# The masks of both halves of a unit's scores in one piece on the vector engine, behind the last score

## The chip, the cores and the metric

The kernel runs on one core of a Trainium2 chip. Its five engines run side by side, each through its own list of instructions: TensorE (PE, with its weight loads shown apart as PEld), VectorE (DVE), ScalarE (ACT), GpSimd (POOL) and SyncE (SP, which issues most DMAs). The metric is the time of one execution on the device, in microseconds (us).

## The reference

Three stages follow one another. The first is a linear recurrence with a complex decay, the second a gated product layer without a nonlinearity, the third eight experts of which each token takes one or none.

```python
def _attn_ref(q, k, v, a_re, a_im):             # (4, 8, 768, 48) each
    mag = np.sqrt(a_re * a_re + a_im * a_im)
    scale = np.minimum(mag, 0.999) / (mag + 1e-06)
    a_re_n, a_im_n = a_re * scale, a_im * scale
    for t in range(S):
        ar, ai = a_re_n[:, :, t, :, None], a_im_n[:, :, t, :, None]
        new_re = ar * S_re - ai * S_im
        new_im = ar * S_im + ai * S_re
        kv = np.einsum('bhd,bhe->bhde', k[:, :, t], v[:, :, t])
        S_re, S_im = new_re + kv, new_im
        y[:, :, t] = np.einsum('bhd,bhde->bhe', q[:, :, t], S_re)
    return y

def _moe_ref(x, w_a, w_b, w_out):               # (3072, 384), 384 x 1536, 1536 x 384
    return (x @ w_a) * (x @ w_b) @ w_out

def _moe2_ref(x, w_skip, w_gate, w1, w2):       # 8 experts, 384 -> 1024 -> 384
    out = x.copy(); do_compute = x @ w_skip > 0; xc = x[do_compute]
    e_idx = np.argmax(xc @ w_gate, axis=1)      # gate_w is the softmax weight of e_idx
    for e in range(E):
        mask = e_idx == e
        y[mask] = gate_w[mask, None] * (np.maximum(xc[mask] @ w1[e], 0.0) @ w2[e])
    out[do_compute] = xc + y
    return out
```

## The kernel before, in words

The recurrence is cut into 24 units: six chunks c of 128 tokens by four batch rows, in the order of `units`. A unit's decays are turned into running products (logarithms on ACT, sums by triangular matmuls `l` on PE, lines L197 and L198, exponentials on ACT), with which q and k are scaled on DVE and POOL (`qr`, `kr`). L323 and L330 transpose them on PE into `pq` and `pk`, which ACT copies into `tq` and `tk`, each in two halves hh of four heads.

`att_run` does the rest of a unit. All its matmuls go through the helper `run` (L368), which ties each to the one before, so their order on PE is fixed among themselves, while other work may stand between them. In order: eight score matmuls of half 0 into `pc`, eight of half 1; the update `ds` of the state, unless c is the last chunk; then `y`, pair of heads by pair: two matmuls with the state (not at c = 0) and two with the masked scores `sc`, the first two pairs from half 0, the last two from half 1. The masks are three DVE instructions for each half: L387 multiplies the right halves of all score blocks by the triangle, L388 the upper left quarter (64 partitions) of the even heads, L389 the lower one of the odd heads; they write `sc0` and `sc1`. A matmul of an even head needs L387 and L388 of its half, one of an odd head needs L389 as well.

The second stage goes on beside it. Two units make a group of 256 tokens, and each group has twelve steps: 18 matmuls `ab` (L562 to L564), a copy on ACT and a product on DVE (`asb`, L568 and L569), a rounded part on ACT and its remainder on DVE (`gh`, `gl`, L571 and L573), and `op` (L545 to L547). The weights of that stage arrive as raw 64-bit words and are decoded at the start, in eighteen chunks (names da, db, do in START): ACT `abs` L431, DVE L432, L436 and L437, ACT L442 and POOL L443.

What sets the order: the program is written in one sequence, and a scheduler with a model of times puts each engine's instructions in order by priority when it builds the kernel; on the chip each engine runs its list in that order and waits with a semaphore where an operand is missing. Three things overrule the scheduler. START lists the steps of the startup, HOLD ties some instructions behind marked ones (the masks are marked ("sc", unit, half)), and whatever is inside `tc.high_priority()`, as the three masks are (L386), is placed as early as its operands allow in that model.

Of the kernel before, what the change touches and what calls it, by code (L numbers as in the profile page):

```python
# [15 lines left out]
ALU = mybir.AluOpType  # L16
AX = mybir.AxisListType

P = 128
# [39 lines left out]
def kern(tc, q, k, v, a_re, a_im, w_a, w_b, w_out, w_skip, w_gate, w1, w2, out):  # L59
    nc = tc.nc  # L60
    dve, act, pool, pe, sync = nc.vector, nc.scalar, nc.gpsimd, nc.tensor, nc.sync
    st = ExitStack()
    with st:
# [13 lines left out]
        def at(name):  # L77
            env.n += 1
            return bank(env.at[env.n % len(env.at)], name, 2)
# [8 lines left out]
        tri = tri_r.bitcast(F32)  # L88
# [15 lines left out]
        for b in range(B):  # L104
            s_ = cpool.tile([96, H * D + 16], F32, name=f"state{b}")
# [16 lines left out]
        tri2 = ew.tile([P, 2, 64], BF16, name="tri2", tag="tri2", bufs=1)  # L122
# [3 lines left out]
        scs = [ew.tile([P, 4, P], F32, name=f"sc{hh}", tag=f"sc{hh}", bufs=1) for hh in range(2)]  # L126
        for s_ in scs:
            s4 = s_.rearrange("s (j x) t -> s j x t", x=2)
# [12 lines left out]
        def after(later, earlier, how=mybir.DependencyClass.NoSync):  # L141
            tc.add_manual_dep(
                later, earlier.name,
                mybir.DependencyInfo(how, mybir.DependencyReason.DATA),
                reason="table order",
            )
# [4 lines left out]
        def mark(key, i):  # L151
            marks[key] = i.ins
            return i
# [143 lines left out]
        def att_pe(i):  # L297
            env.net = None
            att_turn(i)
            att_run(i)  # L300
            env.row = None
# [36 lines left out]
        def att_run(i):  # L338
            c, b = units[i]
            d = U[i]  # L340
            kr, vt, ee = d["kr"], d["v"], d["ee"]
            qT, tks, vp, last, copied = d["turned"]
            if env.net is not None:
                last = env.net
            sc = []
            stt = state[b]

            def delta(run):

                ds = at(f"ds{i}")  # L350
                for h in range(H):
                    for x in range(2):
                        l = d["kf"][:, 96 * h + 64 * x : 96 * h + 64 * x + 64]
                        run(ds[64 * x : 64 * x + 64, h * D : (h + 1) * D], l, vt[:, h * D : (h + 1) * D], start=True, stop=True)
                return ds

            def new_state(ds):
                s3 = stt[:, :W].rearrange("p (h e) -> p h e", e=D)
                d3 = ds[:96, :W].rearrange("p (h e) -> p h e", e=D)
                if c > 0:  # L360
                    dve.tensor_tensor(out=s3, in0=s3, in1=d3, op=ALU.add)
                    d3 = s3
                dve.tensor_tensor(out=s3, in0=d3, in1=ee[:, :, None].to_broadcast([96, H, D]), op=ALU.mult)

            def run(o, l, r, **kw):

                nonlocal last, copied
                ins = pe.matmul(o, l, r, **kw).ins  # L368
                after(ins, last)
                if copied is not None:  # L370
                    after(ins, copied, mybir.DependencyClass.Sync)
                last, copied = ins, None


            for hh in range(2):
                pc = at(f"pc{i}_{hh}")
                for j in range(4):
                    x = j % 2
                    r = qT[hh][:, j * P : (j + 1) * P]
                    for y_ in range(2):  # L380
                        o = 64 * (x ^ y_)
                        run(pc[o : o + 64, j * P + 64 * y_ : (j + 1) * P], tks[hh][:, j * P + 64 * y_ : j * P + 64 * y_ + 64], r[:, 64 * y_ :], start=True, stop=True)
                s_ = scs[hh]
                s4, p4 = (z.rearrange("s (j x) t -> s j x t", x=2) for z in (s_, pc.rearrange("s (j t) -> s j t", t=P)))

                with tc.high_priority():  # L386
                    mark(("sc", i, hh), dve.tensor_tensor(out=s4[:, :, :, 64:], in0=p4[:, :, :, 64:], in1=tri2[:, None].to_broadcast([P, 2, 2, 64]), op=ALU.mult))  # L387
                    dve.tensor_tensor(out=s4[:64, :, 0, :64], in0=p4[:64, :, 0, :64], in1=tri[:64, None, :64].to_broadcast([64, 2, 64]), op=ALU.mult)  # L388
                    dve.tensor_tensor(out=s4[64:, :, 1, :64], in0=p4[64:, :, 1, :64], in1=tri[64:, None, 64:].to_broadcast([64, 2, 64]), op=ALU.mult)  # L389
                sc.append(s_)  # L390
            if c + 1 < NCH:
                ds = delta(run)
            y = at(f"y{i}")
            for pr in range(4):
                o = y[:, pr * P : (pr + 1) * P]
                for inter in (True, False):
                    if inter and c == 0:
                        continue
                    for x in range(2):
                        h = 2 * pr + x  # L400
                        hh, j = h // 4, h % 4
                        if inter:
                            l, r = stt[:, h * D : h * D + 64], qT[hh][:, j * P : (j + 1) * P]
                        else:
                            l, r = (vp[:, pr * D : pr * D + 64] if x else vt[:, h * D : h * D + 64]), sc[hh][:, j]
                        run(o[64 * x : 64 * x + 64], l, r, start=inter or c == 0, stop=not inter)
            g, us = i // 2, slice((i % 2) * P, (i % 2 + 1) * P)
            if i % 2 == 0:
                xts[g] = gpool.tile([P, 4, 2, 2 * P], F32R, tag=f"xt{g % 2}", name=f"xt{g}", bufs=1)
            xt = xts[g]  # L410
            y3 = y.rearrange("e (p t) -> e p t", t=P)
            act.activation(out=xt[:, :, 0, us], in_=y3, func=AF.Copy)
            dve.tensor_tensor(out=xt[:, :, 1, us], in0=y3, in1=xt[:, :, 0, us], op=ALU.subtract)

            xf = xt.bitcast(F32)
            if i % 2:
                for x in range(2):
                    o = 64 * x
                    for j in range(NCC):
                        (pool if x and g in FILLP else sync).dma_start(xf[o + D : o + 64, j], xf[o + 16 * j : o + 16 * j + 16, 3])  # L420
            if c + 1 < NCH:
                new_state(ds)
            env.row = last
            del U[i]
# [543 lines left out]
        for g in range(2, NG):  # L968
            if g + 1 < NG:
                att_exps(g + 1)  # L970
                route(g - 2)
                att_next(g + 1)
                att_trigs(g + 1, False)
            if g == NG - 1:
                ewst.close()
                m2 = ExitStack()
                env.left = m2.enter_context(tc.tile_pool(name="m2l", bufs=1))
                for n in range(NQL):
                    first_q(n)
            u = 2 * g + 2  # L980
            moe1(g, {4: [(att_turn, u)], 6: [(att_run, u), (att_turn, u + 1)], 8: [(att_run, u + 1)]} if g + 1 < NG else {})
            if g == NG - 2:
                table("natural_log_exp_and_others")
            if g >= NG - 2:
                for r in sorted(lgs):
                    route(r)
# [171 lines left out]
```

## Time and profile before

| | |
|---|---|
| median of 3 runs | 891.13 us (890.95 to 892.78) |
| profiled execution | 892.62 us, of which the profile's span is 890.9 us |
| busy PE, PEld | 827.1 us (93%), 788.4 us (88%) |
| busy DVE, ACT, POOL | 571.1 us (64%), 464.4 us (52%), 288.9 us (32%) |
| mean granted clock of TensorE | 0.972 |

A busy share is a mean over stages: the first 160 us, in which weights are decoded and the first units run, are of another kind than the rest. The 1.7 us between the span and the execution's time lie outside what the profiler's rows show.

### The profile page before, as it was taken

What the parts mean: (1) busy time and instruction counts of PE and PEld (TensorE: products, weight loads), DVE (VectorE), ACT (ScalarE), POOL (GpSimd) and SP (SyncE); (2) the same over time, 40 slices, a digit from 0 to 9 for tenths busy, and PEclk for the clock granted to TensorE, in tenths of its full rate; (3) what the DMA queues carried; (4) which work ended last, traced back from release to release, by engine and by line L of the source; (5) the groups of instructions that cost most, each with busy time, mean ns of one, the idle gap of its engine ahead of it and who ended that gap; (6) DMA issues with size and microseconds to landing.
All of it is one profiled execution on the core that took longest, in us unless ns stands there. A gap on an engine that the chain in (4) does not pass through costs nothing. (4 is left out here: it accounts for less than half of the span.)

```text
span 890.9 us, 19279 instructions
## 1 busy us (share of the span) xinstructions
PE 827.1 (93%) x7414; PEld 788.4 (88%) x7414; DVE 571.1 (64%) x1419; ACT 464.4 (52%) x971; POOL 288.9 (32%) x392
## 2 busy tenths in 40 slices
PE   2559798999999999999999999999999999999995
PEld 0448788999999999999989999999999988999995
DVE  4787997848668496674857658575644544755551
ACT  5556665645647374573635646365533425555540
POOL 6247565114131031311113121131302304676751
PEclk9778897999999999999999999999999999999998
DMA  9876872222222131230322313121103209777600
GB/s 163 159 159 104 190 151 54 73 46 72 46 73 55 28 90 30 72 63 19 91 40 63 62 33 86 36 61 22 55 1 98 90 36 311 245 217 231 190 18 30
DMA packets 162804, 81.59 MB, mean 92 GB/s; under 512 B 132788, under 2 KB 148730, under 8 KB 162704
## 3 DMA queue, kind: packets, MB, share of 16 engines
q1 hardware_dynamic: 160656, 74.88, 35.6%
q0 software_dynamic: 2048, 5.40, 1.7%
q8 instruction: 60, 0.98, 0.5%
q14 instruction: 40, 0.33, 0.1%
HBM read 66.10 MB, written 12.61 MB: 88 GB/s over the span
## 5 line engine op out<-in xcount | busy, mean ns | idle before, releaser
L562 PE MATMUL ab<-xt,wa 128*128 128x256 f32 x432 | 128.2, 297 | 3.0 <-DVE asb L569 2.6
L569 DVE TENSOR_TENSOR asb<-ab,asb 128x256 f32<-128x256 f32 x144 | 60.3, 419 | 107.0 <-ACT asb L568 106.7
L563 PE MATMUL ab<-xt,wa 128*128 128x256 f32 x432 | 122.9, 285 | 0.0
L564 PE MATMUL ab<-xt,wa 128*128 128x256 f32 x432 | 122.8, 284 | 0.0
L562 PE MATMUL ab<-xt,wb 128*128 128x256 f32 x432 | 122.5, 283 | 0.0
L563 PE MATMUL ab<-xt,wb 128*128 128x256 f32 x432 | 122.4, 283 | 0.0
L564 PE MATMUL ab<-xt,wb 128*128 128x256 f32 x432 | 122.3, 283 | 0.0
L568 ACT ACTIVATE asb<-ab 128x256 f32<-128x256 f32 x144 | 54.2, 377 | 105.7 <-PE ab L564 104.2
L545 PE MATMUL op<-wo,gl 128*128 128x394 f32 x288 | 101.2, 352 | 2.1 <-DVE gl L573 1.2
L546 PE MATMUL op<-wo,gh 128*128 128x394 f32 x288 | 99.9, 347 | 0.7 <-POOL wo L443 0.7
L547 PE MATMUL op<-wo,gh 128*128 128x394 f32 x288 | 99.6, 346 | 0.0
L571 ACT ACTIVATE gh<-asb 128x256 fp32r<-128x256 f32 x144 | 59.7, 415 | 62.1 <-DVE asb L569 62.0
L573 DVE TENSOR_TENSOR gl<-asb,gh 128x256 fp32r<-128x256 f32 x144 | 67.0, 465 | 33.1 <-ACT gh L571 32.7
L562 PEld LDWEIGHTS ab<-xt,wa 128*128 128x128 f32 x432 | 82.8, 192 | 5.9 <-DVE asb L569 3.3
L563 PEld LDWEIGHTS ab<-xt,wa 128*128 128x128 f32 x432 | 83.1, 192 | 0.1
L564 PEld LDWEIGHTS ab<-xt,wa 128*128 128x128 f32 x432 | 83.1, 192 | 0.0
L562 PEld LDWEIGHTS ab<-xt,wb 128*128 128x128 f32 x432 | 81.9, 190 | 0.1
L563 PEld LDWEIGHTS ab<-xt,wb 128*128 128x128 f32 x432 | 81.9, 190 | 0.0
L564 PEld LDWEIGHTS ab<-xt,wb 128*128 128x128 f32 x432 | 81.9, 189 | 0.0
L809 POOL TENSOR_TENSOR wq<-stg,wq 128x768 fp32r<-128x768 f32 x32 | 59.5, 1864 | 52.2 <-ACT wq L808 29.5
L229 POOL TENSOR_TENSOR ll<-t,lh 128x384 fp32r<-128x384 f32 x20 | 21.4, 1069 | 136.3 <-ACT lh L228 133.0
L847 DVE SCALAR_TENSOR_TENSOR hl<-eh,hh 128x256 fp32r<-128x256 f32 x64 | 27.1, 424 | 51.9 <-ACT hh L846 51.9
(241 smaller groups left out, 2243.9 us busy)
## 6 DMA issues: line engine op xcount, KB each, us to landing
stg<-in_moe_w_dram SPq DMA_DIRECT2D x28, 768.0 KB, 5.2
re<-in_a_re_dram SPq DMA_DIRECT2D x24, 192.0 KB, 2.7
v<-in_v_dram SPq DMA_DIRECT2D x24, 192.0 KB, 2.7
k<-in_k_dram SPq DMA_DIRECT2D x24, 192.0 KB, 4.7
q<-in_q_dram SPq DMA_DIRECT2D x24, 192.0 KB, 3.0
rawo<-in_moe_w_out_dram SPq DMA_DIRECT2D x6, 768.0 KB
xd<-xr SPq DMA_DIRECT2D x24, 192.0 KB, 2.4
out_dram<-xr SPq DMA_DIRECT2D x24, 192.0 KB, 2.0
```

The source lines that it names most:

```text
L545: in_order(pe.matmul(o, gl[:, ts], wh, start=f == 0, stop=False))
L546: pe.matmul(o, gh[:, ts], wl, start=False, stop=False)
L547: i = pe.matmul(o, gh[:, ts], wh, start=False, stop=f == NF - 1)
L562: in_order(pe.matmul(o, wl, xt[:, c, 0], start=c == 0, stop=False))
L563: pe.matmul(o, wh, xt[:, c, 1], start=False, stop=False)
L564: pe.matmul(o, wh, xt[:, c, 0], start=False, stop=c == NCC - 1)
L568: act.activation(out=asb, in_=ab[:, :256], func=AF.Copy)
L569: dve.tensor_tensor(out=asb, in0=ab[:, 256:], in1=asb, op=ALU.mult)
L571: act.activation(out=gh, in_=asb, func=AF.Copy)
L573: dve.tensor_tensor(out=gl, in0=asb, in1=gh, op=ALU.subtract)
L809: lo.tensor_tensor(out=o[:, 1], in0=t, in1=o[:, 0], op=ALU.subtract)
L847: vm = dve.scalar_tensor_tensor(out=gl, in0=o, scalar=0.0, in1=gh, op0=ALU.max, op1=ALU.subtract)
```

## The change

The score matmuls of both halves are collected first (`pcs`); a second loop writes the six masks. The masks lose the high priority, and the first mask of each half gets a dependency with a semaphore on the last of the sixteen score matmuls (`scored`), where before it waited for the last of its own half. The marks for HOLD stay.

```diff
-            sc = []
+            sc, pcs = [], []
...
-                s_ = scs[hh]
+                pcs.append(pc)
+
+            scored = last
+            for hh, (s_, pc) in enumerate(zip(scs, pcs)):
                 s4, p4 = (z.rearrange("s (j x) t -> s j x t", x=2) for z in (s_, pc.rearrange("s (j t) -> s j t", t=P)))
-
-                with tc.high_priority():
-                    mark(("sc", i, hh), dve.tensor_tensor(out=s4[:, :, :, 64:], in0=p4[:, :, :, 64:], in1=tri2[:, None].to_broadcast([P, 2, 2, 64]), op=ALU.mult))
-                    dve.tensor_tensor(out=s4[:64, :, 0, :64], in0=p4[:64, :, 0, :64], in1=tri[:64, None, :64].to_broadcast([64, 2, 64]), op=ALU.mult)
-                    dve.tensor_tensor(out=s4[64:, :, 1, :64], in0=p4[64:, :, 1, :64], in1=tri[64:, None, 64:].to_broadcast([64, 2, 64]), op=ALU.mult)
+                m = mark(("sc", i, hh), dve.tensor_tensor(out=s4[:, :, :, 64:], in0=p4[:, :, :, 64:], in1=tri2[:, None].to_broadcast([P, 2, 2, 64]), op=ALU.mult)).ins
+                after(m, scored, mybir.DependencyClass.Sync)
+                dve.tensor_tensor(out=s4[:64, :, 0, :64], in0=p4[:64, :, 0, :64], in1=tri[:64, None, :64].to_broadcast([64, 2, 64]), op=ALU.mult)
+                dve.tensor_tensor(out=s4[64:, :, 1, :64], in0=p4[64:, :, 1, :64], in1=tri[64:, None, 64:].to_broadcast([64, 2, 64]), op=ALU.mult)
                 sc.append(s_)
```

In the changed kernel the masks are L388, L390 and L391, and every line behind them has a number higher by two.

The scheduler answers with another order of DVE. On DVE, around the masks of unit 14 (pc14), before:

```order
L231 TENSOR_TENSOR im16_5519<-im16_5519,t2_16_6189 128x384
L573 TENSOR_TENSOR gl6_5_5808<-asb6_5_5803,gh6_5_5806 128x256
L569 TENSOR_TENSOR asb6_6_5835<-ab6_6_5810,asb6_6_5835 128x256
L212 TENSOR_SCALAR re18_6305,remin_87<-re18_6305 128x384
L387 TENSOR_TENSOR sc0_112<-pc14_0_5842,tri2_108 128x4x64
L388 TENSOR_TENSOR sc0_112<-pc14_0_5842,tri_r_74 64x2x64
L389 TENSOR_TENSOR sc0_112<-pc14_0_5842,tri_r_74 64x2x64
L220 SCALAR_TENSOR_TENSOR t1_17_6218<-t1_17_6218,t2_17_6219 128x384
L573 TENSOR_TENSOR gl6_6_5840<-asb6_6_5835,gh6_6_5838 128x256
L387 TENSOR_TENSOR sc1_113<-pc14_1_5854,tri2_108 128x4x64
L388 TENSOR_TENSOR sc1_113<-pc14_1_5854,tri_r_74 64x2x64
L389 TENSOR_TENSOR sc1_113<-pc14_1_5854,tri_r_74 64x2x64
```

and at the same place in the changed kernel:

```order
L220 SCALAR_TENSOR_TENSOR t1_17_6218<-t1_17_6218,t2_17_6219 128x384
L575 TENSOR_TENSOR gl6_5_5808<-asb6_5_5803,gh6_5_5806 128x256
L231 TENSOR_TENSOR im16_5519<-im16_5519,t2_16_6189 128x384
L571 TENSOR_TENSOR asb6_6_5835<-ab6_6_5810,asb6_6_5835 128x256
L212 TENSOR_SCALAR re18_6305,remin_87<-re18_6305 128x384
L388 TENSOR_TENSOR sc0_112<-pc14_0_5842,tri2_108 128x4x64
L390 TENSOR_TENSOR sc0_112<-pc14_0_5842,tri_r_74 64x2x64
L391 TENSOR_TENSOR sc0_112<-pc14_0_5842,tri_r_74 64x2x64
L388 TENSOR_TENSOR sc1_113<-pc14_1_5851,tri2_108 128x4x64
L390 TENSOR_TENSOR sc1_113<-pc14_1_5851,tri_r_74 64x2x64
L391 TENSOR_TENSOR sc1_113<-pc14_1_5851,tri_r_74 64x2x64
L231 TENSOR_TENSOR im17_5530<-im17_5530,t2_17_6219 128x384
```

The step L220 of unit 17 has gone from between the halves to a place ahead of both, and gl6_6 has gone behind both (it is the row after the last one shown). Units 10 and 18 change in the same way; in units 8, 12 and 16 L220 stood ahead of sc0 before, and only gl goes from between the halves to behind them. In unit 6 and in the odd units from 5 on both halves stood together before, and nothing between them changes; but on PE, in the odd units 7 to 19, a pair of the triangular matmuls `l` (L197, L198) now stands in the middle of y, ahead of its first matmul on sc1, where it stood behind y.

The second place is in the startup, on DVE around the masks of unit 3 (pc3), where the last chunks of weights are decoded (decb5 and deca5). Before:

```order
L436 SCALAR_TENSOR_TENSOR decb5_1425<-rawb5_1290,decb5_1425 128x768
L387 TENSOR_TENSOR sc0_112<-pc3_0_941,tri2_108 128x4x64
L388 TENSOR_TENSOR sc0_112<-pc3_0_941,tri_r_74 64x2x64
L389 TENSOR_TENSOR sc0_112<-pc3_0_941,tri_r_74 64x2x64
L437 SCALAR_TENSOR_TENSOR decb5_1425<-rawb5_1290,decb5_1425 128x768
L387 TENSOR_TENSOR sc1_113<-pc3_1_953,tri2_108 128x4x64
L388 TENSOR_TENSOR sc1_113<-pc3_1_953,tri_r_74 64x2x64
L389 TENSOR_TENSOR sc1_113<-pc3_1_953,tri_r_74 64x2x64
L432 TENSOR_SCALAR deca5_1417<-deca5_1417 128x768
L212 TENSOR_SCALAR re7_2239,remin_87<-re7_2239 128x384
L569 TENSOR_TENSOR asb0_9_1347<-ab0_9_1322,asb0_9_1347 128x256
L436 SCALAR_TENSOR_TENSOR deca5_1417<-rawa5_1244,deca5_1417 128x768
```

and in the changed kernel, from the second half's masks on:

```order
L388 TENSOR_TENSOR sc1_113<-pc3_1_950,tri2_108 128x4x64
L390 TENSOR_TENSOR sc1_113<-pc3_1_950,tri_r_74 64x2x64
L391 TENSOR_TENSOR sc1_113<-pc3_1_950,tri_r_74 64x2x64
L508 COPY w2s4_1299<-wt4_1_1310 128x10
L439 SCALAR_TENSOR_TENSOR decb5_1425<-rawb5_1290,decb5_1425 128x768
L434 TENSOR_SCALAR deca5_1417<-deca5_1417 128x768
L571 TENSOR_TENSOR asb0_9_1347<-ab0_9_1322,asb0_9_1347 128x256
L212 TENSOR_SCALAR re7_2239,remin_87<-re7_2239 128x384
L438 SCALAR_TENSOR_TENSOR deca5_1417<-rawa5_1244,deca5_1417 128x768
L571 TENSOR_TENSOR asb0_8_1410<-ab0_8_1385,asb0_8_1410 128x256
L575 TENSOR_TENSOR gl0_9_1352<-asb0_9_1347,gh0_9_1350 128x256
L439 SCALAR_TENSOR_TENSOR deca5_1417<-rawa5_1244,deca5_1417 128x768
```

The last step of decb5 (L437, now L439) stands behind both halves of the masks, and asb0_8 stands ahead of gl0_9. The row of deca5's last step has the same number in both lists, 176. On PE, y of unit 3 is followed by six `op` matmuls on gl0_9 in both lists; the six on gl0_8 stood behind the first `ab` of the last weights before and stand ahead of it now.

The third place is in a unit of the last chunk, unit 20 (pc20), on DVE. Before:

```order
L569 TENSOR_TENSOR asb9_6_8193<-ab9_6_8168,asb9_6_8193 128x256
L387 TENSOR_TENSOR sc0_112<-pc20_0_8200,tri2_108 128x4x64
L388 TENSOR_TENSOR sc0_112<-pc20_0_8200,tri_r_74 64x2x64
L389 TENSOR_TENSOR sc0_112<-pc20_0_8200,tri_r_74 64x2x64
L573 TENSOR_TENSOR gl9_6_8198<-asb9_6_8193,gh9_6_8196 128x256
L387 TENSOR_TENSOR sc1_113<-pc20_1_8212,tri2_108 128x4x64
```

and in the changed kernel:

```order
L571 TENSOR_TENSOR asb9_6_8193<-ab9_6_8168,asb9_6_8193 128x256
L575 TENSOR_TENSOR gl9_6_8198<-asb9_6_8193,gh9_6_8196 128x256
L388 TENSOR_TENSOR sc0_112<-pc20_0_8200,tri2_108 128x4x64
L390 TENSOR_TENSOR sc0_112<-pc20_0_8200,tri_r_74 64x2x64
L391 TENSOR_TENSOR sc0_112<-pc20_0_8200,tri_r_74 64x2x64
L388 TENSOR_TENSOR sc1_113<-pc20_1_8209,tri2_108 128x4x64
```

Here gl9_6 went from between the halves to a place ahead of them. On PE the list of unit 20 keeps its order: scores, state part of y, score part of y.

## Rows read from the trace of the kernel before

**Rows 1.** Busy time by stretch: start:end, length, each engine, PEclk, DMA share, GB/s.
```profile
120.00:140.00 20.00, 15.39 (x166) 14.29 (x166) 19.19 (x30) 12.46 (x26) 13.86 (x16) 0.96 0.62 110
138.20:148.40 10.20, 9.03 (x37) 8.96 (x37) 6.54 (x11) 6.07 (x14) 6.46 (x12) 0.50 0.34 70
160.00:700.00 540.00, 537.11 (x5268) 516.78 (x5267) 353.37 (x1009) 288.86 (x635) 116.14 (x195) 1.00 0.24 57
```

**Rows 2.** Waits of PE, 160 to 700: total us, times, longest.
```profile
PE y L368 <- DVE sc L388: 1.9, 6, 0.5
```

**Rows 3.** Timeline of DVE, unit 14: start, length, line; brackets: idle before it.
```profile
445.98 0.56 DVE L231 TENSOR_TENSOR im<-im,t 128x384 f32<-128x384 f32 x1 [1.12 <-ACT t L162]
447.85 0.42 DVE L387 TENSOR_TENSOR sc<-pc,tri 128x256 f32<-128x256 f32 x1
...
448.82 0.56 DVE L220 SCALAR_TENSOR_TENSOR t<-t,t 128x384 f32<-128x384 f32 x1
449.30 0.42 DVE L573 TENSOR_TENSOR gl<-asb,gh 128x256 fp32r<-128x256 f32 x1
449.73 0.42 DVE L387 TENSOR_TENSOR sc<-pc,tri 128x256 f32<-128x256 f32 x1
```

**Rows 4.** Timeline of PE in y of units 10, 14 and 18.
```profile
340.53 0.39 PE L368 MATMUL y<-tq,state 96*64 96x128 f32 x4
341.27 0.43 PE L368 MATMUL y<-sc,v 128*64 128x128 f32 x2 [0.35 <-DVE sc L388]
...
450.40 0.43 PE L368 MATMUL y<-sc,v 128*64 128x128 f32 x2 [0.46 <-DVE sc L388]
...
558.06 0.43 PE L368 MATMUL y<-sc,v 128*64 128x128 f32 x2 [0.32 <-DVE sc L388]
```

**Rows 5.** Timeline of PE, then DVE, unit 9.
```profile
299.49 0.28 PE L368 MATMUL y<-sc,v 128*64 128x128 f32 x1
```
```profile
298.54 0.29 DVE L389 TENSOR_TENSOR sc<-pc,tri_r 64x128 f32<-64x128 f32 x1
```

**Rows 6.** Timeline of PE, then DVE, unit 20.
```profile
607.92 1.56 PE L368 MATMUL pc<-tq,tk 96*64 96x128 f32 x32
609.54 0.43 PE L368 MATMUL y<-sc,v 128*64 128x128 f32 x2
```
```profile
608.87 0.42 DVE L387 TENSOR_TENSOR sc<-pc,tri 128x256 f32<-128x256 f32 x1 [1.07 <-PE pc L368]
609.21 0.27 DVE L388 TENSOR_TENSOR sc<-pc,tri_r 64x128 f32<-64x128 f32 x1
```

**Rows 7.** Timeline of DVE, then POOL, then PE, end of the startup.
```profile
132.50 2.47 DVE L437 SCALAR_TENSOR_TENSOR decb<-rawb,decb 128x768 int32<-128x768 int32 x1
135.96 0.57 DVE L432 TENSOR_SCALAR deca<-deca 128x768 int32<-128x768 int32 x1
137.37 1.68 DVE L436 SCALAR_TENSOR_TENSOR deca<-rawa,deca 128x768 int32<-128x768 int32 x1
138.97 0.41 DVE L573 TENSOR_TENSOR gl<-asb,gh 128x256 fp32r<-128x256 f32 x1
139.77 0.94 DVE L437 SCALAR_TENSOR_TENSOR deca<-rawa,deca 128x768 int32<-128x768 int32 x1
```
```profile
132.48 1.68 POOL L443 TENSOR_TENSOR wo<-deco,wo 128x768 fp32r<-128x768 f32 x1
136.08 2.15 POOL L443 TENSOR_TENSOR wb<-decb,wb 128x768 fp32r<-128x768 f32 x1
```
```profile
136.07 0.29 PE L368 MATMUL y<-sc,v 128*64 128x128 f32 x1 [2.36 <-DVE sc L389]
...
139.44 0.70 PE L545 MATMUL op<-wo,gl 128*128 128x394 f32 x1 [1.17 <-DVE gl L573]
```

## Prediction

> **What bounds the kernel now.** I read the busy time by stretch first [rows 1]. From 160 to 700 us PE is busy 537.11 of 540 us at a granted clock of 1.00: 2.9 us are all that any change of order can take out there, apart from matmuls that are issued late without leaving PE idle. The reader should see DVE beside it, 353.37 us, with room. In the startup it is the other way about: from 120 to 140 DVE is busy 19.19 of 20 us and PE 15.39, and from 138.2 to 148.4 PE works at 0.50, the lower of its two levels (1.2 GHz), after it had stood idle before 136.07 and again before 139.44 [rows 7]. Next come the waits of PE: in the long stretch the masked scores hold y six times, 1.9 us in total [rows 2]. Then the timelines, around one unit of each kind.
>
> **The even units, where other work stood between the halves.** In unit 14 sc0's first mask starts at 447.85, then L220 at 448.82 and gl at 449.30 run, and sc1's first mask starts only at 449.73 [rows 3]. PE waits 0.46 us for it, before 450.40; unit 10 shows 0.35 and unit 18 0.32 [rows 4]. These three are the idle time that the change can take: 1.13 us. PE loses more than that, since matmuls overlap: in unit 10 the four on the state start at 340.53 and their row lasts 0.39, but the next could have been issued before its end. I estimate 0.15 for each such place, 0.45 together, and another 0.3 for units 8, 12 and 16, where only gl stood between and PE shows no idle. Sum: 1.9 us gained. sc1's masks then start 0.9 us earlier in relation to sc0's, twice the wait, so none of it should be left. The step L220 (0.56 us) now stands ahead of sc0. If it fits into idle time of DVE ahead of it, as the 1.12 us before 445.98, it costs nothing; if not, sc0 is later by its 0.5 us to the next start, three times 0.5 us. So this term lies between -2.0 and 0, and I take -1.9, as the 1.12 us are twice L220. gl goes behind sc1, about 1 us later; the `op` that reads it comes behind y and other work, which is its cover. Without it each of the six units loses up to 1 us.
>
> **The odd units.** The masks now wait for the last score of both halves. In unit 20 the 16 scores start at 607.92 and sc0's mask at 608.87, while DVE was waiting for just that [rows 6]; half of the scores takes 0.67 us (half of the 1.56 less the overlap of the last), so sc0 starts 0.67 later wherever DVE stands ready. In an odd unit `ds` lies between the scores and y. In unit 9 L389 starts at 298.54 and would start at 299.21 and end at 299.50; the even head's matmul of y started at 299.49, the odd head's right behind it [rows 5]. A matmul starts about 0.06 after its mask (sc1 of unit 14: L388 follows L387 by 0.34 and lasts 0.27, from 449.73 that is 450.34, and the matmul starts at 450.40). So the odd head is 0.06 late; eight units make 0.5 us. sc1's masks follow sc0's at 0.97, later than before in relation to y by the same 0.67; the pair of `l` matmuls that now stands in y ahead of sc1 covers that, and in unit 5, without the pair, up to 0.1 is open. Bounds: 0 and 8 x 0.2 = 1.6; I take 0.5.
>
> **The last chunk, units 20 to 23.** Here there is no `ds`. In unit 20 y on sc0 starts at 609.54, and L388 ended at 609.48 [rows 6]: no slack. With the first mask at 609.54, L388 ends 0.34 + 0.27 later, at 610.15, and y goes on at 610.21: 0.67 lost. Unit 22 has the same pattern; units 21 and 23 have a little other work between, and I put them at 0.3 and 0.55. Sum 2.2 us, bounds 1.3 (20 and 22 alone) and 2.7 (four times 0.67).
>
> **The startup.** Unit 3's sc1 masks were ready late because the decode step L437 stood ahead and took 2.47 us, against 0.94 for the same step at 139.77 [rows 7]. It ran beside POOL's L443 from 132.48, which lasted 1.68: L437 began its own 0.94 about when POOL was done. With both masks ahead of it, y no longer waits 2.36 us before 136.07. What is late next: behind y stands `op` on gl0_9, which waited until 139.44 for gl at 138.97, and gl stands behind deca5's L436. In the new order L437 starts at about 133.65 (two halves of masks and a copy from 131.56), is held until POOL ends at 134.16 and ends near 135.1; L432 follows there and not at 135.96. L436 could then start at 136.5. But POOL's L443 for wb runs from 136.08 to 138.23, and L436 lasted 1.68 from 137.37, that is to 0.82 behind POOL's end. If that repeats, L436 ends at 139.05 whenever it starts after 136.08, then asb0_8 and gl0_9 follow, and `op` is 0.3 later than before. If L436 comes ahead of POOL, it is done by 137.4 and gl0_9 1.3 earlier. From `op` on PE is busy without a gap (the 1.17 us before it are all the idle time of 138.2 to 148.4 [rows 1, 7]), so the end of the startup moves as `op` does: -1.3 to +0.3, and I take 0, nearer to the row in which POOL comes first. To that comes the clock: the stretch at 0.50 costs 10.2 x 0.5 = 5.1 us of full speed; if the gap lies elsewhere the stretch may become shorter or longer, and I allow a third of it, 1.7 us, either way.
>
> On that contention the Trainium skill ("SBUF — State Buffer", section "SBUF: two separate sides") says that VectorE and GpSimd share a pair of ports as an exclusive lock: an operation with two SBUF inputs and a GpSimd operation that reads SBUF block each other for a whole instruction. The 2.47 us agree with it: 1.68 less 0.02, plus 0.94, would be 2.60. The masks have one input in PSUM, so by the rule they can run beside POOL; and L436, two inputs in SBUF, can't, which speaks against a gain here, as the sum above has it.
>
> **Sum.** -1.9 + 0.5 + 2.2 + 0 = +0.8 us on the profiled execution of 892.62 (span 890.9 and 1.7 outside): 893.4. That execution lies 1.5 above the median of 891.13, so the forecast in terms of the median is 891.9.
>
> **Rivals.**
> Faster: L436 gets ahead of POOL's L443. The 1.3 us and 1.7 us of half clock come off, and the last chunk costs only its lower bound. -1.9 + 0.5 + 1.3 - 3.0 = -3.1: 888.0. For it speaks the large wait that disappears at 136.07, against it the row in which L436 is held by POOL.
>
> Slower: L220 of the odd units, placed ahead of gl, im and both masks on DVE, waits for ACT, and everything queued behind it in order (gl, asb, sc0, sc1) waits too; y waits behind sc0, and the `ab` step behind asb. The place is units 10, 14 and 18, the price 0.5 to 1 us each in place of the gain: with 0.5 the term is +1.5 instead of -1.9, the sum 1.5 + 0.5 + 2.2 = +4.2, and 895.3. It decides as soon as L220's wait is longer than the 1.12 us that DVE idled. For it speaks that this idle time is itself a wait for ACT; against it that ACT is busy only about half of the time.
>
> No effect of its own: most units had both halves together already, and in the others gain and loss meet near 891.1. That lies inside the forecast's own range.
>
> **How the numbers follow.** A change under 0.2% (1.8 us) can't be told from none, that is 889.35 to 892.9. The forecast, with its neighbours, gets 0.41 (0.37 of it inside these bounds, 0.02 beyond either) and its own range is 889 to 893.5. The faster rival gets 0.31, the slower one 0.24, and 0.04 goes to the startup alone at +1.7 and more. From these: faster 0.33, same 0.37, slower 0.30. The range reaches half way into either rival: 887.8 to 895.
>
> **What would show it.** Right: no wait of y on sc1 in units 10, 14 and 18; y on sc0 0.67 later after the scores in units 20 and 22; no wait before y of unit 3, but a longer one of `op` on gl0_9; L436 of deca5 beside POOL again above 1.5 us. Wrong: waits of y on sc0 in even units behind L220, a startup that ends by more than 2 us earlier or later, or PE idle in the odd units' y.

## The result, and the profile after

The changed kernel is slower: 897.68 us (median of 8 runs, 894.51 to 901.0) against 891.5 (8 runs, 889.73 to 894.3); the ratio is 1.0065, 95% interval 1.0044 to 1.0086, that is 3.9 to 7.7 us. The prediction had 891.9 us and a range up to 895. The profiled execution took 898.57 us, its span is 896.8 against 890.9.

Lining up the start of the same matmul in both traces shows where the 5.9 us between the spans arise. The first score matmul of a unit is a good mark; behind the units there are the steps of the last group and the first matmuls `eh` of an expert. lg is DVE's copy of a group's routing columns out of what `op` wrote:

| mark | before | after | later by | where it arose |
|---|---|---|---|---|
| unit 4, first score | 172.30 | 172.22 | -0.08 | startup: -0.1 |
| unit 6 | 230.09 | 231.12 | 1.03 | units 4 and 5: +1.1 |
| unit 8 | 283.80 | 285.37 | 1.57 | units 6 and 7: +0.5 |
| unit 20 | 607.92 | 609.14 | 1.22 | units 8 to 19: -0.35 |
| twelfth group, its first `ab` | 687.47 | 691.60 | 4.13 | units 20 to 23: +2.9 |
| its seventh step, first `ab` | 708.03 | 712.95 | 4.93 | +0.8, of which 0.6 is a wait for lg |
| second expert, first `eh` | 755.42 | 761.64 | 6.22 | +1.3, of which 1.2 is the clock |

The last row is not the change's. Behind 744.3 TensorE ran 3.4 us at its lower level in the profiled execution of the changed kernel, and not in that of the kernel before. Of the twelve traces of this document, whose lists are the same in that stage, eight show it and four don't, and from the first `eh` of the first expert to that of the second those eight take 1.2 to 1.4 us longer. Busy time by stretch, before and then after (columns as in [rows 1]; the first expert starts at 739.7 before and at 744.7 after, so the two pairs of rows show the same work):

```profile
735.00:740.00 5.00, 2.78 (x21) 1.93 (x20) 0.88 (x2) 0.98 (x2) 3.63 (x9) 1.00 0.59 156
740.00:745.00 5.00, 5.00 (x40) 4.92 (x39) 1.50 (x4) 1.15 (x3) 0.00 (x0) 1.00 0.92 312
```
```profile
740.00:745.00 5.00, 2.70 (x20) 1.88 (x18) 0.88 (x2) 0.98 (x2) 3.56 (x9) 0.93 0.63 162
745.00:750.00 5.00, 5.00 (x31) 5.00 (x31) 1.09 (x3) 1.16 (x4) 0.00 (x0) 0.72 0.97 339
```

Nor is the row above it shown to be the change's. The kernels' lists are the same from the twelfth group on, and this stretch of 20.56 us before and 21.35 after took 20.23 to 22.79 in the twelve traces: 21.32, with the same wait, in the run that leaves the last chunk as it was, and 20.39, without a wait of `op` for lg, in one that has the whole change in it. PE in the first of these two:

```profile
PE op L558 <- DVE lg L597: 1.6, 1, 1.6
```

The stretches and the waits of PE that answer to [rows 1, 2], after (the second wait, 1.0 before, is the one for lg):

```profile
138.20:148.40 10.20, 7.54 (x32) 7.54 (x33) 6.52 (x13) 4.94 (x10) 6.42 (x11) 0.67 0.16 35
160.00:700.00 540.00, 537.10 (x5240) 513.37 (x5238) 347.67 (x988) 287.34 (x630) 114.35 (x193) 1.00 0.24 55
```
```profile
PE y L368 <- DVE sc L390: 2.3, 5, 0.7
PE op L547 <- DVE lg L586: 1.6, 1, 1.6
```

The lesson is in the second row: PE is as busy as before, 537.10 of 540 us, and has got less far (5240 matmuls against 5268). Most of the loss is not idle time but matmuls that are issued further apart, and a busy share can't show that. By the marks, units 4 to 7 lose their 1.6 us without any more idle time; in units 20 to 23 PE waits 1.45 us for the masks, half of the 2.9; and in units 8 to 19 its idle time falls by 0.85.

**Even units.** DVE in unit 14, which answers to [rows 3]:

```profile
447.40 0.96 DVE L220 SCALAR_TENSOR_TENSOR t<-t,t 128x384 f32<-128x384 f32 x1 [1.22 <-ACT t L162]
448.28 0.41 DVE L575 TENSOR_TENSOR gl<-asb,gh 128x256 fp32r<-128x256 f32 x1
448.62 0.55 DVE L231 TENSOR_TENSOR im<-im,t 128x384 f32<-128x384 f32 x1
449.08 0.41 DVE L571 TENSOR_TENSOR asb<-ab,asb 128x256 f32<-128x256 f32 x1
449.42 0.54 DVE L212 TENSOR_SCALAR_CACHE_REDUCE re<-re 128x384 f32<-128x384 f32 x1
449.89 0.08 DVE L212 DVE_READ_ACCUMULATOR re<-re 128x1 f32 x1
449.89 0.41 DVE L388 TENSOR_TENSOR sc<-pc,tri 128x256 f32<-128x256 f32 x1
...
450.85 0.42 DVE L388 TENSOR_TENSOR sc<-pc,tri 128x256 f32<-128x256 f32 x1
```

The first masks of the halves start 0.96 apart, and sc1 is waited for no more; but sc0 starts 1.43 behind the last score (448.46) and y waits 0.70 for it. The idle 1.22 us stand right ahead of L220, as a wait for ACT.

**Odd units.** PE in unit 9, which answers to [rows 5]:

```profile
300.61 0.28 PE L368 MATMUL y<-sc,v 128*64 128x128 f32 x1
300.68 0.32 PE L368 MATMUL y<-sc,vp 128*64 128x128 f32 x1
...
301.39 0.39 PE L368 MATMUL y<-tq,state 96*64 96x128 f32 x3
301.70 0.45 PE L197 MATMUL l<-ll,tri_r 128*128 128x384 f32 x1
301.99 0.33 PE L198 MATMUL l<-lh,tri_r 128*128 128x384 f32 x1
302.25 0.32 PE L368 MATMUL y<-sc,v 128*64 128x128 f32 x1
302.26 0.32 PE L368 MATMUL y<-sc,vp 128*64 128x128 f32 x1
302.41 0.27 PE L368 MATMUL y<-sc,v 128*64 128x128 f32 x1
```

Before, y<-sc,v and y<-sc,vp (even and odd head) started within 0.01 of each other all through y, pair behind pair at 0.10 to 0.12. Now the odd head comes 0.07 later, as forecast, but the two heads stay out of step up to the l pair: from the first matmul of y to the last one ahead of that place are 1.13 us, against 1.02 before. Behind the l pair they start together again. And the l pair costs more here than elsewhere: 0.29 between its two matmuls, 0.26 to the next one of y and 0.16 to the one behind, where among `op` matmuls one follows another at 0.18.

**Last chunk.** DVE, then PE in unit 20, which answer to [rows 6]:

```profile
609.97 1.02 DVE L575 TENSOR_TENSOR gl<-asb,gh 128x256 fp32r<-128x256 f32 x1 [0.96 <-ACT gh L573]
610.92 0.41 DVE L388 TENSOR_TENSOR sc<-pc,tri 128x256 f32<-128x256 f32 x1
611.25 0.27 DVE L390 TENSOR_TENSOR sc<-pc,tri_r 64x128 f32<-64x128 f32 x1
```
```profile
611.58 0.43 PE L368 MATMUL y<-sc,v 128*64 128x128 f32 x2 [0.66 <-DVE sc L390]
```

The scores start at 609.14, sc0 1.78 later, against 0.95 before: the 0.67 of the forecast and 0.16 behind gl. Here PE does wait.

**Startup.** DVE, POOL and PE, which answer to [rows 7]:

```profile
134.87 1.32 DVE L439 SCALAR_TENSOR_TENSOR decb<-rawb,decb 128x768 int32<-128x768 int32 x1
...
138.19 1.96 DVE L438 SCALAR_TENSOR_TENSOR deca<-rawa,deca 128x768 int32<-128x768 int32 x1
140.40 0.41 DVE L575 TENSOR_TENSOR gl<-asb,gh 128x256 fp32r<-128x256 f32 x1
```
```profile
134.35 1.02 POOL L229 TENSOR_TENSOR ll<-t,lh 128x384 fp32r<-128x384 f32 x1
...
137.52 1.81 POOL L445 TENSOR_TENSOR wb<-decb,wb 128x768 fp32r<-128x768 f32 x1
```
```profile
140.86 0.70 PE L547 MATMUL op<-wo,gl 128*128 128x394 f32 x1 [2.82 <-DVE gl L575]
```

y of unit 3 no longer waits, `op` waits 2.82 us for gl instead, and L438 ends 0.82 behind POOL again (140.15 against 139.33), just as it did before. `op` is 1.4 later, but more of its stretch runs at full clock (0.67 against 0.50 from 138.2 to 148.4), and unit 4 starts where it did.

### The profile page after: what moved, and what is told of

It is laid out like the page before. It is cut to its first block, busy times and chain, and to the rows that moved or that the text cites. A ratio compares the mean times of both kernels' runs of the same rounds, so it can differ in the third digit from the quotient of the medians.

```text
span 896.8 us, 19286 instructions
## 1 busy us (share of the span) xinstructions
PE 830.2 (93%) x7414; PEld 787.3 (88%) x7414; DVE 570.7 (64%) x1419; ACT 465.5 (52%) x971; POOL 290.5 (32%) x392
## 5 line engine op out<-in xcount | busy, mean ns | idle before, releaser
L571 DVE TENSOR_TENSOR asb<-ab,asb 128x256 f32<-128x256 f32 x144 | 60.2, 418 | 99.5 <-ACT asb L570 98.7
```

Source lines behind the costliest of these rows:

```text
L571: dve.tensor_tensor(out=asb, in0=ab[:, 256:], in1=asb, op=ALU.mult)
```

## The experiments

After the traces I held theory A: the even units gain by the single piece of their masks, the odd units and units 4 and 5 lose because the scheduler puts other work into the middle of y, and the last chunk loses because nothing lies between its scores and y. Against it stood B, that DVE's new order or the late masks cost in themselves, and C, that startup and clock made the difference by chance. D, that the even units gain by an l pair that comes earlier and not by their masks, came later, when the first runs had taken down a part of A.

Each kernel was run in five rounds against the kernel before. "Block" is the time from the first score matmul of a unit to the start of the last matmul of y, worked out from each trace's timeline:

| kernel | ratio (95%) | unit 9 | unit 10 | unit 14 | unit 18 | unit 20 | unit 23 |
|---|---|---|---|---|---|---|---|
| before | 1 | 3.98 | 4.87 | 5.92 | 4.84 | 4.15 | 3.51 |
| changed | 1.0065 (1.0044 to 1.0086) | 4.79 | 4.18 | 5.31 | 4.18 | 4.97 | 4.18 |
| even units only | 0.9998 (0.9986 to 1.0010) | 3.99 | 4.74 | 5.85 | 4.75 | 4.14 | 3.51 |
| odd units only | 0.9998 (0.9984 to 1.0012) | 4.79 | 4.32 | 4.31 | 4.32 | 4.15 | 3.51 |
| changed, l not in y | 1.0050 (1.0037 to 1.0064) | 4.18 | 4.83 | 4.84 | 4.84 | 4.81 | 4.18 |
| last chunk only | 1.0043 (1.0030 to 1.0056) | 3.99 | 4.83 | 4.77 | 4.84 | 4.81 | 4.18 |
| units 4 and 5 only | 1.0014 (1.0003 to 1.0025) | 3.99 | 4.89 | 4.88 | 4.93 | 4.15 | 3.51 |
| last chunk, half the delay | 1.0022 (1.0005 to 1.0040) | 3.99 | 4.90 | 4.81 | 4.80 | 4.81 | 3.85 |
| masks as before, l behind y | 0.9919 (0.9902 to 0.9936) | 3.99 | 3.99 | 3.98 | 3.99 | 4.14 | 3.51 |
| the same, one piece in 6 to 19 | 0.9942 (0.9923 to 0.9960) | 4.18 | 4.18 | 4.18 | 4.18 | 4.14 | 3.51 |
| masks as before, l inside y | 1.0007 (0.9989 to 1.0025) | 5.47 | 3.99 | 3.98 | 3.99 | 4.14 | 3.51 |
| changed, last chunk as before | 1.0025 (1.0013 to 1.0037) | 4.79 | 4.19 | 5.29 | 4.19 | 4.15 | 3.52 |

Unit 14 of before contains a chance of 1.1 us: where the same lists ran again (last chunk only, units 4 and 5 only, half the delay) it took 4.77 to 4.88. Of that the trace shows 0.17 as a wait of DVE for a DMA (L212, on `re`). I count differences in unit 14 only from 4.8 on. It bears on the marks too: from unit 8 to unit 20 those three traces take 322.88 to 323.60 us, the profiled execution of before 324.12 and that of the changed kernel 323.77. So the -0.35 in the table of marks can be anything from there to +0.9, and is +0.2 against the mean of the four.

One thing needs no run. Without the line with the dependency (`after(m, scored, ...)`), with or without the high priority, the scheduler builds the same lists on PE and DVE as for the kernel before. So neither the second loop nor the lost priority does anything: the whole effect is the dependency on the last score.

**Even units only.** The masks are written by a function, used in place where a unit keeps the order of before, and behind the scores where `one` is true:

```diff
+            one = i % 2 == 0 and 6 <= i < 20
...
+                if not one:
+                    with tc.high_priority():
+                        masks(hh, pc)
+            if one:
+                scored = last
+                for hh in range(2):
+                    masks(hh, pcs[hh], scored)
```

> Only the even units 6 to 18 get their six masks in one piece behind the last score; all other units keep the order of before (startup, odd units, last chunk). Theory A (the change gains in the even units, and loses because in other units PE work of another kind is pushed into the middle of y, and because the last chunk has nothing between scores and y): blocks of units 8 to 18 shorten as in the changed kernel, 3.7 us in all, odd units stay at 4.25 us, so about 887.5 us against 891. Rival B (the vector engine's order is what costs: L220 ahead of the masks holds up the steps behind it): the blocks shorten but the time between them grows by as much, 891 us or more. Rival C (the slower time is the startup's clock, by chance): 891, no different from before.

Measured: 892.44 against 892.61 us, no difference. The even blocks from 8 to 18 became 0.65 us shorter in all, where theory A wanted 3.7. My first theory fell here: the gain that the changed kernel shows in its even units is not the masks' piece. DVE in unit 10 of this run, and the step on ACT that L220 waits for:

```profile
337.44 0.56 DVE L231 TENSOR_TENSOR im<-im,t 128x384 f32<-128x384 f32 x1 [1.13 <-ACT t L162]
...
339.24 0.56 DVE L220 SCALAR_TENSOR_TENSOR t<-t,t 128x384 f32<-128x384 f32 x1
339.71 0.42 DVE L586 TENSOR_TENSOR gl<-asb,gh 128x256 fp32r<-128x256 f32 x1
340.04 0.42 DVE L380 TENSOR_TENSOR sc<-pc,tri 128x256 f32<-128x256 f32 x1
```
```profile
337.88 0.60 ACT L162 ACTIVATE t<-t,b_eps 128x384 f32<-128x384 f32 x1
```

What stood between the halves now stands ahead of both: the wait has gone from sc1 to sc0, where y waits 0.13, 1.24 and 0.14 us in units 10, 14 and 18. L220 did not fit into the idle 1.13 us, because that is a wait for the same chain of ACT and DVE steps: it ends at 337.44, and the exponential that L220 reads ends at 338.48. The time between the blocks did not grow, so rival B is no better.

**Odd units only.** `one = i % 2 == 1 and 6 <= i < 20`.

> Only the odd units 7 to 19 get their masks in one piece behind the last score, and the pair of l matmuls goes into the middle of their y as in the changed kernel; all others as before. Theory A: each odd unit costs 0.58 us, seven of them 4.1 us, about 895 us. The term of the prediction (0.06 us a unit): 0.5 us, 891.5. Rival C (startup clock): 891.

Measured: 893.17 against 892.61, no difference, and not the 4 us that theory A wanted. The odd blocks did grow by 0.8, but the even blocks, whose code is that of before, fell to 4.32. The even units' gain comes from the odd units' change.

**The whole change, l not in y.** The first matmul of an l pair depends on the last one of y:

```diff
+            first = pe.matmul(o[:, :W], tri_r, lo, start=True, stop=False)
+            if i is not None and i >= 6 and env.row is not None:
+                after(first.ins, env.row)
```

> The whole change, but the first matmul of each l pair from unit 6 on depends on the last matmul of the y that was written before it, so that no l pair stands in the middle of y. Theory A: the part of the odd units' loss that is the change of work in the middle of y goes, 0.35 us for each of 7 odd units and about 0.7 in unit 21, so 3 us less than the changed kernel, about 894.5; the odd blocks are then about 4.45 us (4.25, the broken pairing of even and odd heads 0.11, and a wait for sc1 of up to 0.1). Rival B (the late masks themselves cost the 0.58, the l pair only fills the wait): without the l pair PE stands idle there instead, and the time stays at 897.5.

Measured: 897.67 against 892.61 (ratio 1.0050), as slow as the changed kernel within the noise, and not the 894.5 of the expectation. Odd blocks fell to 4.18, less than the 4.45 forecast, without any idle PE; but the even blocks went back to 4.8. Half of the expectation held (the l pair in y costs), and what it left out is that the early l pair also gives something.

**Last chunk only.** `one = i >= 20`.

> Only the last chunk, units 20 to 23, gets its masks in one piece behind the last score; everything ahead of 607 us is as before. Theory A: 2.9 us are lost between the scores of unit 20 and y of unit 23, and 0.8 more at the wait of op for the routing's lg near 700, so 3.7 us: about 895. The prediction's term: 2.2 us, 893.5. Rival C: nothing, 891.

Measured: 896.22 against 892.61, by the ratio +3.8 us (2.7 to 5.0), as expected of theory A and not of rival C. In its trace units 20 to 23 take 2.7 us more; the 0.55 behind them, at lg, is within what that stretch does anyway. The blocks of units 20, 22 and 23 are 0.67 longer (forecast 0.67, 0.67 and 0.55), and that of 21 by 0.92: there the matmuls `pp` of the routing go into the middle of y.

**Units 4 and 5 only.** `one = i in (4, 5)`.

> Only units 4 and 5 get their masks in one piece behind the last score; the startup ahead of 172 us and everything from unit 6 on are as before. In the order, ab matmuls then stand in the middle of y of both units, as in the changed kernel. Theory A' (work of another kind in the middle of y costs for each change there and back): the blocks of units 4 and 5 are about 1.0 and 2.0 us longer, and between unit 4's scores and the first ab of unit 6's group 1.1 us are lost net, the rest being only ab work that is done earlier; about 1.1 us slower than before. If the pieces are only moved: 0.

Measured: 893.40 against 892.21, by the ratio +1.25 us (0.3 to 2.2), as expected; the blocks are 6.24 and 5.95 against 5.29 and 3.99, most of it work that is only done earlier: in relation to unit 4, unit 6 starts 0.9 later than before. What it looks like, PE in unit 4 of the changed kernel:

```profile
176.17 0.28 PE L565 MATMUL ab<-xt,wa 128*128 128x256 f32 x1
176.38 0.43 PE L368 MATMUL y<-sc,v 128*64 128x128 f32 x2
176.74 0.38 PE L566 MATMUL ab<-xt,wa 128*128 128x256 f32 x1
177.05 0.32 PE L368 MATMUL y<-sc,vp 128*64 128x128 f32 x1
```

From the lone `ab` matmul to the next one of y are 0.31 us; among its own kind it takes 0.12.

**Last chunk, half the delay.** sc0's mask waits for the fourth score of half 1:

```diff
+                    if hh == 1 and j == 1:
+                        middle = last
...
+                    masks(hh, pcs[hh], scored if hh else middle)
```

> As the run with the last chunk alone, but sc0's first mask waits for the fourth of half 1's eight score matmuls and not for the eighth; sc1's waits for the eighth as there. If the loss of the last chunk is the delay of sc0's mask behind the scores (0.67 us a unit there), half the delay gives about 0.33 us in each of four units, 1.3 us, and about half of the 0.6 at lg: 1.3 to 1.9 us slower than before. If it is the lost priority or the order of the list, or the wait in itself, the loss stays at 3.3 to 3.9 us.

Measured: 893.00 against 892.21, by the ratio +2.0 us (0.5 to 3.6). Units 22 and 23 lose 0.33 each, half of 0.67; 20, where gl stands between sc0's masks in DVE's list, still loses 0.66, and 21 nothing. In all units 20 to 23 take 1.4 us more than before, against 2.7 with the whole delay. The loss falls with the delay; the wide interval alone would not show that, the blocks do.

**Masks as before, l behind y.** In the kernel before, only the l pairs of units 8 to 21 change:

```diff
-                cumsum(l2, hi, lo)
+                if 8 <= i < 22:
+                    with tc.high_priority():
+                        cumsum(l2, hi, lo, env.row)
+                else:
+                    cumsum(l2, hi, lo)
```

`cumsum` makes its first matmul depend on the last argument, the last matmul of the y written before.

> The masks exactly as before (own half's last score, high priority); only the l pairs of units 8 to 21 are changed: they get the high priority and stand right behind the last matmul of y of the odd unit ahead. Theory D (in the changed kernel the even units became faster because the l pair, and behind it the chain of ACT and DVE work of the next units, came earlier, not because the masks stand together): even blocks fall from 4.6 to 5.2 us (5.9 in unit 14) to 4.2 to 4.4 with odd ones at 3.98, and the kernel is 2 to 4 us faster than before. Theory A (the gain is the masks' single piece): the even blocks change by less than 0.2 us and the time stays at that of before.

Measured: 885.11 against 892.21, ratio 0.9919 (0.9902 to 0.9936): faster than both kernels, and by more than expected. All blocks from 8 to 19 are 3.98 or 3.99. The pairs are not all that moves: the scheduler's order of DVE and ACT changes with them. DVE in unit 10:

```profile
337.44 0.42 DVE L588 TENSOR_TENSOR asb<-ab,asb 128x256 f32<-128x256 f32 x1 [1.22 <-ACT asb L587]
338.35 0.42 DVE L592 TENSOR_TENSOR gl<-asb,gh 128x256 fp32r<-128x256 f32 x1 [0.48 <-ACT gh L590]
338.88 0.42 DVE L386 TENSOR_TENSOR sc<-pc,tri 128x256 f32<-128x256 f32 x1
...
339.85 0.42 DVE L386 TENSOR_TENSOR sc<-pc,tri 128x256 f32<-128x256 f32 x1
```

No decay step is near the masks: the two steps L220 (here L222) ran at 327.95 and 329.01, against 334.95 and 339.24 in the run with the even units alone. The exponentials behind the l pairs tell why, ACT in the run with the even units alone and then in this one:

```profile
312.00 1.64 ACT L162 ACTIVATE t<-l 128x384 f32<-128x384 f32 x4
```
```profile
302.72 1.64 ACT L162 ACTIVATE t<-l 128x384 f32<-128x384 f32 x4
```

**The same, masks of 6 to 19 in one piece.**

> The run with the l pairs right behind y (885.1 us, ratio 0.992), and in units 6 to 19 the masks in one piece behind the last score; the other units as before. This shows what the one piece does by itself where nothing stands between the halves. If the delayed masks cost only what the run without l pairs in y showed (odd blocks 4.18 against 3.98, by a broken pairing of even and odd heads), odd and even blocks grow by 0.2 us each, 14 units: 2.8 us more than that run, about 888. If the one piece gains in the even units, as the prediction had it: the same as that run or up to 2 us faster.

Measured: 886.72 against 892.36, ratio 0.9942. The ratios differ by 0.0023, about 2 us, but the intervals overlap; in the traces all blocks from 8 to 19 are 4.18 to 4.19, 0.20 longer, and from unit 7 to unit 20 it loses 2.7 us on the run above. By itself the one piece only costs here, by the blocks as much as expected; the two times alone would not show it.

**Masks as before, l inside y.** High priority for the pairs, without the dependency on y.

> As the run with the l pairs right behind y, with the high priority but without the dependency on the last matmul of y: one pair now stands inside ds and one inside y of every odd unit from 7 to 19; the even units' order is the same. The work is the same, so the difference is the price of going to other work and back in the middle of a unit's block: in the changed kernel the odd block was 0.8 us longer with one pair in y (0.2 of it the broken pairing), against 0.36 for the same pair among op matmuls, so 0.2 to 0.3 net for each pair, two pairs, seven units: 3 to 4 us slower than the run with the pairs behind y. If only the earlier start of the pairs matters: no difference.

Measured: 892.05 against 892.36, no better than before, and 7 us slower than with the pairs behind y by the medians. The odd blocks are 5.47, 1.48 longer, of which 0.72 is the four matmuls at 0.18 that are only moved: 0.38 for each pair and 5.3 us over seven units, more than the 3 to 4 expected. The even blocks are 3.99 as with the pairs behind y, so it is the earlier pairs that free them, wherever these stand.

**The change without the last chunk.** `one = i < 20`.

> The changed kernel, but units 20 to 23 have their masks as before. If the terms add up, it is faster than the changed kernel by what the last chunk alone cost (3.8 us by the medians, 3.3 in the trace), and still 1 to 2 us slower than before, by units 4, 5 and 7: a ratio of 1.001 to 1.002. If the terms don't add up (the startup or the clock decides), it stays nearer to 1.0065.

Measured: 894.45 against 892.21, by the ratio +2.2 us (1.2 to 3.3). With the 3.8 us of the last chunk alone that makes 6.0, and the whole change cost 5.8: the terms add up, within intervals of 2 us.

## Why the prediction was wrong

**Even units, forecast -1.9: the step that failed.** I wrote that L220 fits into the idle 1.12 us of DVE [rows 3]. With the masks of the even units alone in one piece it did not: the idle time was a wait within the chain that ends in L220, and sc0 became late by what sc1 gained. The gain was nothing, which was an end of my range for the term. What the even units gain in the changed kernel, 2.7 to 3.8 us from even to odd starts of units 8 to 19, came from the l pairs. The three waits of [rows 4] were not all, either: the six of [rows 2] have one of 0.24 in unit 6, one of 0.16 in unit 12, which I took to show none, and one for sc0 in unit 14, of 0.40.

**Odd units, forecast +0.5.** 3.4 to 3.6 us in units 9 to 19. I let the l pair in y cover the wait for free. Without it PE showed no wait to cover, and it costs 0.34 net (0.81 less 0.11 for the heads out of step and the 0.36 that are only moved). The odd head was late by 0.07, as forecast, but that put the heads out of step, at 0.11 a unit up to the l pair and 0.20 where no l pair ends it. That the two terms nearly cancelled (about +0.2 over units 8 to 19) is one cause: one pair that moves forward both breaks y and frees the next unit's masks. The sum of my two terms was -1.4, so about 1.6 us were missing.

**Units 4 to 7: +1.6.** Unit 4 stood in no term, and units 5 and 7 only with 0.06 each. I had looked at the masks there and not at what the scheduler put between the scores and y: `ab` matmuls in units 4 and 5, the l pair in unit 7. The list of PE showed it.

**Last chunk, forecast +2.2: +2.9.** The mechanism was right; unit 21 was missized (0.92 and not 0.3). Unit 20 cost 0.82, with gl ahead of the masks, but 0.66 in the run with the last chunk alone, which has gl at the same place.

**Startup, forecast 0 with a range of -1.3 to +0.3 for `op`.** Its end came out at -0.1. One trace can't settle this term: the nine whose lists are the same up to unit 4 reach it between 170.5 and 173.7, in the mean at 172.4; the three with the startup of the changed kernel do so at 172.2, 172.5 and 172.9. So it is near the forecast 0, as far as such a spread can tell. `op` was 1.4 late, outside my range, as POOL came to wb 1.44 later (137.52 against 136.08); that L436 ends 0.82 behind POOL's wb held to the hundredth, in a different place. What the Trainium skill ("SBUF — State Buffer", section "SBUF: two separate sides") says of the lock agrees with this trace too: the masks ran at 0.42 beside POOL's wo (132.08 for 2.33), while L439 took 1.32 beside POOL's ll, and L438 1.96 beside wb, each ending 0.82 behind it. With POOL idle L439 took 0.94 (140.73).

**The rivals.** The slower rival named the right place, L220 ahead of both halves, and its wait in unit 14 was 1.22 us, longer than the 1.12 that was to decide. Its price would have been y waiting in units 10, 14 and 18; y waited in one of them (unit 14, 0.70), as the l pairs had come earlier. In the run with the even units alone it waited in all three. The faster rival's POOL race was lost.

**The bound.** The prediction began with 2.9 us that an order could take out, apart from matmuls that are issued late without leaving PE idle. That exception is larger than the rule: with the l pairs behind y units 8 to 19 took 316.90 us, 6.0 to 7.2 less than with the lists of before, of which PE had been idle for 1.7 in the trace of before.

What the terms have to meet is the ratio of the runs, 5.8 us (3.9 to 7.7). 1.6 + 0.2 + 2.9 make 4.7, inside that interval. Of the 3.9 us between this and the forecast of 0.8, units 4 to 7 and units 8 to 19 make 1.6 each and the last chunk 0.7. Whether the rest is noise or a loss that these marks don't show stays open; the clock near 745 and the stretch at lg, which differ between the two profiled executions, are not shown to belong to it.

## What to carry to other kernels

When an order is built by a scheduler, an added wait is paid for where the scheduler fills it: look on PE's list for what is put into the middle of a run of small paired matmuls, and price each visit there and back (here 0.34 to 0.38 us). A wait ahead of a DVE step names a chain; ask what starts that chain, since moving its first link (here four matmuls, nine us earlier) was worth more than any order around its last one. And a stage in which PE is 99.5% busy can still lose time.

## What was not expected of the hardware

Matmuls of 64 columns for an even and an odd head that write the lower and the upper 64 partitions start within 0.01 us of each other, pair behind pair at 0.10 to 0.12. Once one is 0.07 late the two stay out of step until other work comes between, or to the end of y; that costs 0.11 and 0.20 us in a block of 4 us. Going from such matmuls to full ones and back costs 0.34 to 0.38 us for a pair of 128x384, net of the 0.36 that the pair takes among its like. Of the clock: whether TensorE falls to its lower level near 745 differs from one profiled execution to the next (eight of twelve), in kernels whose work there is the same.
